# Attention, MoE and routed MoE on one core: the place of the raw weight loads in the attention's load order, and of the routing constants

## The chip, the cores and the metric

One core of one Trainium2 chip. The metric is the device time of one execution in microseconds, as the median of three runs.

## The reference

Three layers follow each other. The attention has 32 heads of 576 rows and 64 columns, with a decay that is a running sum of log f, and a causal mask. Its output, 2304 tokens of 512, goes through a gated MLP ("the first MoE" in the code's names), and that through a routed MoE with eight experts, in which each token goes to one expert.

```python
scores = scale * np.matmul(q, k.transpose(0, 1, 3, 2))
decay = cum[:, :, :, None] - cum[:, :, None, :]
scores = np.where(causal, -1000000000.0, scores + decay)
...
g = x @ w_gate
silu = g * (1.0 / (1.0 + np.exp(-g)))
val = x @ w_val
return (silu * val @ w_out).astype(np.float32)
...
logits = x @ w_gate
e_idx = np.argmax(logits, axis=1)
...
h = np.maximum(x[mask] @ w1[e], 0.0)
ye = h @ w2[e]
out[mask] = gate_w[mask, None] * eom[mask, e, None] * ye
```

## The kernel before, in words

The kernel has three stages on one core. From 0 to about 184 us the attention runs, in 16 pairs of heads; then the first MoE in steps of 384 tokens by 256 hidden columns; from about 680 us on the routing and the eight experts.

In the attention the order of work on every engine is written out by hand, in the table ORDER (lines 38 to 48). Each engine's line is one turn; `Attention.run` (line 346) repeats it once for each pair. An entry such as `qk 1 3` is the operation, the pair relative to the turn, and a tile number: the scores of the next pair, tile 3. TensorE multiplies q and k into PSUM (`qk`, line 164, tiles 4 to 0 in two buffers ps_s), VectorE adds the mask and takes the row maximum (`ttr`, line 180, which empties the PSUM buffer), ScalarE takes the exponential (`exp`, line 188), GpSimd and VectorE make the reciprocal of the row sum (`add`, `rec`, `mul`, lines 196 to 205), TensorE turns the weights (`tr`, line 226), ScalarE and VectorE copy the result (`cp`, lines 235 and 237, tile th), and TensorE multiplies by v (`av`, line 262). VectorE copies the output to xt (line 278); GpSimd splits it into two parts (lines 290 and 288). Every engine works strictly in its order, and so does the queue of SP, which issues the loads.

An entry of the SP line with `> x` is a load that must not be issued before the operation x is done: a hand-made tie that spreads the loads over the turn. `rows` loads rows of the decay (dk, line 142), `load p 0` to `3` are four loads of q and k of a pair (line 132, 144 KB each), `vload` two of v (line 139). q and k are loaded three turns ahead of the pair's own, and their first product is `qk 2 4`, late in the next turn.

The weights of the first MoE come as 64-bit numbers and are decoded to 32 bits on the chip. The first six raw pieces of 512 KB are decoded within the attention, one in every second turn, beginning with the turn of pair 2 (H0). Their loads are `fetch 0 0` to `3`, four quarters of 128 KB each (`quarter`, line 427, tile raw). In the turn after, VectorE does `d0` (line 456) behind the copy `cp 0 0 0`, and `d1` (line 458) at the end; in the turn behind that VectorE does `d2` (460) and ScalarE `sq` (464), and GpSimd finishes (`ts`, `pm1`, `pm2`, lines 466 to 472; `pm3`, 474, a turn later). The later pieces are decoded in the first MoE (`decode`, lines 443 to 448, fetched at line 431).

The routing constants are one tile cst. `Consts.rest` (line 1032) loads 237 KB of it, and `Consts.split` (lines 1036 and 1037) casts two of its 128x128 parts to tile uo on VectorE. They are used by `Route.chunk`, in the last group of the first MoE. In the kernel before, the hook of the first fetch calls `rest`, and that of the first `d0` calls `split`.

In the first MoE each step i has two halves f: `gv` (lines 510 to 518: two products, Tanh, and VectorE's hs and hl), and `g2` (lines 528 to 534: the product ps_y, added to y by VectorE).

Of the kernel before, what the change touches and what calls it, by code (L numbers as in the profile page):

```python
# [33 lines left out]
NP = B * H // 2  # L34
# [7 lines left out]
    DVE="rec 0 1, cp 0 0 0, d2 0, d0 0, ttr 1 3 1, ttr 1 2 1, ttr 1 3 0, ttr 1 2 0, cp 0 1 0, xt -1, "  # L42
        "ttr 1 0 0, ttr 1 1 0, ttr 1 0 1, ttr 1 1 1, cp 0 2 1, rec 1 0, d1 0, ttr 2 4 0, ttr 2 4 1",
    POOL="mul 0 1, sub -2, pm3 -1, ts -1, pm1 0, add 1 0, pm2 0, mul 1 0, add 1 1, cast -1",
    SP="rows 2, load 3 0 > cp 0 0 1, load 3 1 > exp 1 3 1, fetch 0 0 > cp 0 1 1, fetch 0 1 > exp 1 2 1, "
       "load 3 2 > exp 1 3 0, vload 1 0 > cp 0 2 0, fetch 0 2 > exp 1 0 1, vload 1 1 > exp 1 1 1, "
       "load 3 3 > exp 1 0 0, fetch 0 3 > exp 2 4 0",
)
ENG = mybir.EngineType
SYNC = mybir.DependencyInfo(mybir.DependencyClass.Sync, mybir.DependencyReason.DATA)  # L50
# [7 lines left out]
class Attention:  # L58
# [287 lines left out]
    def run(self, hook, pool):  # L346
# [31 lines left out]
        for q in queue.values():  # L378
            q[:] = [o for o in q if o not in done]
        with self.tc.manual_schedule(engines={ENG.PE, ENG.Activation, ENG.DVE, ENG.Pool, ENG.SP}):  # L380
            self.decay(*dec)
# [658 lines left out]
def tile_kernel(tc, io, out, dbg=None):  # L1040
    nc = tc.nc
    with ExitStack() as ctx:
        pool = lambda cx, nm, b=1, **k: cx.enter_context(tc.tile_pool(name=nm, bufs=b, **k))
        cp = pool(ctx, "cst")
        dr = pool(ctx, "dram", space=DRAM)
        per = dict(sb=cp, sb2=cp, dram=dr)
        cst = Consts(nc, cp, io["cst"])
        wts = Weights(nc)
        wts.pools.append(pool(ctx, "wA", 6))
        with ExitStack() as c1:  # L1050
            xp = pool(c1, "x")
            xth = xp.tile([128, 4, N], F32R, name="xth")
            xtl = xp.tile([128, 4, N], F32R, name="xtl")
            raw = pool(c1, "raw", 2)
            tmp = pool(c1, "dtmp", 1)
            m1 = MoE1(tc, c1, cst, io, wts, raw, tmp, xth, xtl)
            with ExitStack() as ca:
                cst.attention(pool(ca, "acst"))
                at = Attention(tc, ca, cst, io, xth, xtl)

                todo, raws = [], {}

                def hook(k, p, j=0):
                    n = (p - H0 - DEC[k]) // 2
                    if k == "fetch":
                        if n == 0 and j == 0:
                            cst.rest()
                            todo.extend(m1.parts(0))
                        if j == 0:
                            raws[n] = raw.tile([128, 1024], I32, name="raw")  # L1070
                        return m1.quarter(raws[n], todo[n][0], j)
                    else:
                        if k == "d0" and n == 0:
                            cst.split()
                        m1.piece(k, raws[n], *todo[n][1:])

                at.run(hook, wts.pools[0])
            m1.open(c1)
            wab = [wts.pools[0], pool(c1, "wB", 6)]
            slp = pool(c1, "slots", space=PSUM)  # L1080
            slots = slp.tile([128, 512], F32, name="slots")
            rt = Route(tc, c1, cst, io, per, m1.y)
            gates = rt.gates(pool(c1, "gtmp"))
            CH = [(384 * i, 384) for i in range(6)]
            CL = CH[:4] + [(1536 + 256 * i, 256) for i in range(3)]
            steps = [(g, t0, n) for g in range(6) for t0, n in (CL if g == 5 else CH)]
            for i in range(len(steps) + 1):
                for f in range(2):
                    if i < len(steps):
                        g, t0, n = steps[i]  # L1090
                        if g < 5 and t0 == 0 and f == 0:
                            wts.pools = [wab[(g + 1) % 2]]
                            if g:
                                m1.load(g + 1)
                        if (i, f) in ((3, 0), (8, 0)):
                            with tc.issue_after(m1.mark[0].ins), tc.issue_after(m1.mark[1].ins):
                                next(gates, None)
                        if i == 1 and f == 0:
                            wts.pools = [wab[1]]
                            todo[:] = m1.parts(1)  # L1100
                        if 2 * i + f in HALF:
                            src, hi, lo = todo.pop(0)
                            with tc.issue_after(m1.mark[0].ins), tc.issue_after(m1.mark[1].ins):
                                m1.decode(m1.fetch(src), hi, lo)
                        if g == 5 and t0 == CH[2][0] and f == 0:
                            wts.pools = [wab[0]]
                            w00 = load_expert(nc, io, wts, raw, 0, 0)
                        m1.gv(g, t0, n, f)
                    if i:
                        for d in (2 * f, 2 * f + 1):  # L1110
                            m1.g2(*steps[i - 1], d)
                if i and steps[i - 1][0] == 5:
                    rt.chunk(*steps[i - 1][1:], slots)
            info = rt.finish(slots)
        with ExitStack() as c2:
            wc = pool(c2, "wC", 12, reuse_waits="tile")
            wts.pools = [wab[0], wc, wc]
            m2 = MoE2(tc, c2, cst, io, wts, rt.yd, rt.gd, info, out)
            pblk = pool(c2, "blk")
            m2.braw = pool(c2, "blk_raw")  # L1120
            cur = cp.tile([128, 1], F32, name="cur")
            nc.vector.memset(cur, 0.0)
            gwk = pool(c2, "gwk")
            m2.L[0, 0] = w00
            with tc.issue_after(rt.mark[0].ins), tc.issue_after(rt.mark[1].ins):
                m2.pull(0)
                m2.warm(WARM[0], info["id1"])
                for t in range(NSB):
                    m2.pre(0, t)
                    m2.warm(WARM[1 + t], m2.YG[0][min(t, 1)])  # L1130
            with tc.issue_after(m2.mark[0].ins), tc.issue_after(m2.mark[1].ins):
                for u in range(1, 4):
                    m2.L[0, u] = load_expert(nc, io, wts, m2.raw, 0, u)
            st = [(e, u) for e in range(E_) for u in range(4)]
            blk = m2.block(pblk, cur, rt, True)
            with tc.manual_schedule(engines={mybir.EngineType.Pool}):
                for i, (e, u) in enumerate(st):
                    if (u == 0 if e else u == P0) and e + 1 < E_:
                        m2.pull(e + 1)
                    if e == 1 and u == 0:  # L1140
                        m2.gates(0)
                    if e and u == 3:
                        m2.gates(e)
                    if i in BLK0:
                        next(blk)
                    m2.g1(e, u)
                    if i == GI:
                        rt.gate_rows(m2.ps_g, gwk)
                        rt.blocks(info, gwk)
                    if u >= P1 and u < P1 + NSB and e + 1 < E_:  # L1150
                        m2.pre(e + 1, u - P1)
                    if i in BLK1:
                        with tc.issue_after(m2.hmark[0].ins), tc.issue_after(m2.hmark[1].ins):
                            next(blk)
                    if i:
                        m2.g2(*st[i - 1])
                    if u < NSB and e:
                        m2.put(e - 1, u)
                    if (e, u) == (6, 3):
                        for _ in blk:  # L1160
                            pass
                nc.gpsimd.drain()
                m2.g2(*st[-1])
                for t in range(NSB):
                    m2.put(E_ - 1, t)
            trip = nc.values_load(info["trip"][0:1, 0:1], min_val=0, max_val=NOB + E_)
            with tc.For_i(0, trip, 1):
                for _ in m2.block(pblk, cur, rt, False):
                    pass
# [35 lines left out]
```

## Time and profile before

| what | value |
|---|---|
| median of 3 runs | 941.75 us (940.64 to 949.98) |
| the profiled execution's own time | 939.82 us |
| its span, first to last instruction | 938.0 us |
| TensorE (PE) busy | 898.9 us, 96% |
| VectorE (DVE) busy | 576.4 us, 61% |
| ScalarE (ACT) busy | 401.0 us, 43% |
| GpSimd (POOL) busy | 242.0 us, 26% |

The busy share of TensorE is an average over the three stages, and TensorE's idle time is not spread evenly; the stretches say where it lies. A wait's row tells which engine stood, at which line, for whom, how long in total, how often and how long at most. In a timeline a row is one or more instructions of a kind; a bracket at the end is the idle time of that engine just before, and what ended it.

### The profile page before, as it was taken

The page shows a single profiled execution, that of the slowest core. Times are in us where ns is not written, and L with a number is a line of the kernel's source. Part 1 is how long each engine was busy: PE and PEld are TensorE (multiplying, and loading weights), DVE is VectorE, ACT ScalarE, POOL GpSimd, SP SyncE. Part 2 cuts the span into 40 slices and gives each one's busy share as a digit, 9 for nine tenths or more (in the row PEclk, how much of TensorE's full clock was granted, in tenths as well). Part 3 has the DMA queues.
Part 4 walks back from the last instruction along what each step waited for, and adds up shares of the span by engine and source line. Part 5 has one row for each costly group of instructions (what it writes and reads, how often), then busy time and mean ns, then how long its engine had stood idle before and what let it go on. Part 6 is the DMA issues. An engine that isn't in the chain of part 4 may idle for free.

```text
span 938.0 us, 23689 instructions
## 1 busy us (share of the span) xinstructions
PE 898.9 (96%) x9848; PEld 862.9 (92%) x9848; DVE 576.4 (61%) x1355; ACT 401.0 (43%) x874; POOL 242.0 (26%) x249
## 2 busy tenths in 40 slices
PE   8988888999999999999999999999899999999995
PEld 6877778899999999999999999999699999999995
DVE  6767776555784396487466445767875556466421
ACT  6766776444431231132132122333365555555421
POOL 2355555711120030020021000000212655155222
PEclk9999999999999999999999999999899999999998
DMA  4433333112230030021021000101595775566300
GB/s 124 137 112 103 107 105 113 51 46 68 70 111 1 1 113 23 1 91 46 1 68 46 1 1 1 68 34 65 177 300 157 234 238 188 172 197 199 114 34 30
DMA packets 59975, 87.87 MB, mean 94 GB/s; under 512 B 7080, under 2 KB 39322, under 8 KB 59867
## 3 DMA queue, kind: packets, MB, share of 16 engines
q1 hardware_dynamic: 54363, 72.17, 25.0%
q0 software_dynamic: 5504, 14.17, 4.3%
q8 instruction: 78, 1.28, 0.5%
q14 instruction: 30, 0.25, 0.1%
HBM read 76.76 MB, written 10.08 MB: 93 GB/s over the span
## 4 chain that ended last, share of the span: by engine, by line
PE 72%; DVE 10%; issue 9%; DMA 4%; POOL 3%; ACT 2%; POOLq 0%; SPq 0%; DVEq 0%; ACTq 0%
PE ps_g L510 27%; PE ps_y L528 14%; PE m_psy L832 8%; PE m_psg L817 7%; PE ps_s L164 4%; PE ps_t L226 4%; PE avx L262 3%; DVE dt L443 2%; DVE e L180 2%; DMA raw<-w 1%; PE rt_ps L668 1%; POOL w L448 1%; POOL out L858 1%; PE m_pst L782 1%; PE m_pst L848 1%
## 5 line engine op out<-in xcount | busy, mean ns | idle before, releaser
L510 PE MATMUL ps_g<-xth,w 128*128 128x384 f32 (+1 forms) x1184 | 309.0, 331 | 0.0
L510 PEld LDWEIGHTS ps_g<-xth,w 128*128 128x128 f32 x1184 | 213.1, 188 | 0.9
L510 PE MATMUL ps_g<-xtl,w 128*128 128x384 f32 (+1 forms) x592 | 196.0, 331 | 0.0
L528 PE MATMUL ps_y<-hh,w 128*128 128x384 f32 (+1 forms) x592 | 160.6, 332 | 2.2 <-DVE y L534 2.2
L817 PE MATMUL m_psg<-ygh,w 128*128 128x304 f32 x512 | 115.1, 307 | 0.4 <-ACT ygh L784 0.4
L832 PE MATMUL m_psy<-h2h,w 128*128 128x304 f32 x512 | 114.6, 306 | 0.0
L448 POOL TENSOR_TENSOR w<-ds,w 128x512 fp32r<-128x512 f32 x30 | 41.6, 1386 | 273.7 <-ACT w L447 273.7
L510 PEld LDWEIGHTS ps_g<-xtl,w 128*128 128x128 f32 x592 | 111.3, 188 | 0.0
L528 PEld LDWEIGHTS ps_y<-hh,w 128*128 128x128 f32 x592 | 107.0, 188 | 4.3 <-DVE y L534 4.0
L188 ACT ACTIVATE e<-e,mx 64x64 f32<-64x64 f32 (+4 forms) x160 | 88.1, 552 | 38.9 <-DVE mx L180 37.9
L744 DVE TENSOR_TENSOR w<-raw,w 128x1024 fp32r<-128x1024 f32 x64 | 76.6, 1222 | 38.0 <-ACT w L743 20.6
L528 PE MATMUL ps_y<-hl,w 128*128 128x384 f32 (+1 forms) x296 | 97.8, 330 | 0.0
L517 ACT ACTIVATE hh<-hs 128x384 fp32r<-128x384 f32 (+1 forms) x74 | 38.2, 516 | 135.9 <-DVE hs L516 135.9
L515 DVE SCALAR_TENSOR_TENSOR hs<-hs,ps_g 128x384 f32<-128x384 f32 (+1 forms) x74 | 40.0, 540 | 83.5 <-ACT hs L514 83.5
L817 PEld LDWEIGHTS m_psg<-ygh,w 128*128 128x128 f32 x512 | 85.5, 189 | 0.6 <-ACT ygh L784 0.5
L832 PEld LDWEIGHTS m_psy<-h2h,w 128*128 128x128 f32 x512 | 85.6, 188 | 0.4
L743 ACT ACTIVATE w<-raw 128x1024 fp32r<-128x1024 f32 x64 | 67.5, 1058 | 39.9 <-PE m_psg L817 17.7
L180 DVE CUSTOM_DVE_ANT_0 e<-ps_s,mask 128x576 f32<-128x576 f32 (+4 forms) x160 | 69.5, 482 | 24.2 <-PE ps_s L164 24.1
L514 ACT ACTIVATE hs<-ps_g 128x384 f32<-128x384 f32 (+1 forms) x74 | 35.4, 478 | 107.2 <-PE ps_g L510 107.1
L534 DVE TENSOR_TENSOR y<-ps_y,y 128x384 f32<-128x384 f32 (+1 forms) x124 | 67.0, 541 | 19.1 <-PE ps_y L528 18.2
L798 POOL DMA_INDIRECT yg<-yd,sl_idx x24 | 27.9, 1163 | 193.6 <-DVE sl_idx L704 168.3
L832 PE MATMUL m_psy<-h2l,w 128*128 128x304 f32 x256 | 77.4, 302 | 0.0
(302 smaller groups left out, 1572.5 us busy)
## 6 DMA issues: line engine op xcount, KB each, us to landing
raw<-w SPq DMA_DIRECT2D x64, 512.0 KB
qk<-qk SPq DMA_DIRECT2D x64, 144.0 KB
raw<-mg SPq DMA_DIRECT2D x10, 512.0 KB
raw<-mv SPq DMA_DIRECT2D x10, 512.0 KB
raw<-mo SPq DMA_DIRECT2D x10, 512.0 KB
yd<-yr SPq DMA_DIRECT2D x18, 256.0 KB
v<-vL SPq DMA_DIRECT2D x16, 160.0 KB
v<-vL SPq DMA_DIRECT2D x16, 128.0 KB
```

Source lines behind the costliest of these rows:

```text
L180: self.nc.vector.tensor_tensor_reduce(out=o, in0=x, in1=y, scale=-0.125, scalar=BIGF, op0=ALU.add, op1=ALU.min, accum_out=mx[:m])
L188: return self.nc.scalar.activation(e, e, ACTF.Exp, bias=self.M.pop((p, i, a))[:m], scale=-1.0, accum_out=self.rs[p % 2][:m, c:c + 1])
L448: nc.gpsimd.tensor_sub(lo, s3, hi.bitcast(F32))
L510: nc.tensor.matmul(ps[:, :n], w[:, k, fs], x[:, k], start=(k == 0 and c == 0), stop=(k == 3 and c == 2))
L515: nc.vector.scalar_tensor_tensor(s[:, :n], s[:, :n], 1.0, pss[0][:, :n], op0=ALU.add, op1=ALU.mult)
L517: a = nc.scalar.activation(hh[:, f, :n], s[:, :n], ACTF.Copy)
L528: nc.tensor.matmul(ps[:, :n], w[:, f, ds], h[:, f, :n], start=(f == 0 and c == 0), stop=(f == 1 and c == 2))
L534: nc.vector.tensor_add(y, ps[:, :n], y)
L743: nc.scalar.activation(hi, r, ACTF.Copy)
L744: nc.vector.tensor_sub(lo, r, hi.bitcast(F32))
L817: nc.tensor.matmul(ps[:, :C], w[:, k, fs], x[:, k], start=(k == 0 and c == 0), stop=(k == 3 and c == 2))
L832: nc.tensor.matmul(self.P[e][d][:, :C], w[:, f, ds], h[:, f], start=(u == 0 and f == 0 and c == 0), stop=(u == 3 and f == 1 and c == 2))
```

## The change

The line of SP in ORDER is written in another order and with other ties: the four quarters of a raw piece stand directly behind `rows`, with the last one tied to `exp 1 2 1`; q's and k's loads and v's stand between and behind them. The load of the constants (`rest`) moves to step 2, second half, of the first MoE, with a dependence on the last load of v; their casts (`split`) move to step 9.

```diff
-    SP="rows 2, load 3 0 > cp 0 0 1, load 3 1 > exp 1 3 1, fetch 0 0 > cp 0 1 1, fetch 0 1 > exp 1 2 1, "
-       "load 3 2 > exp 1 3 0, vload 1 0 > cp 0 2 0, fetch 0 2 > exp 1 0 1, vload 1 1 > exp 1 1 1, "
-       "load 3 3 > exp 1 0 0, fetch 0 3 > exp 2 4 0",
+    SP="rows 2, fetch 0 0 > cp 0 0 1, fetch 0 1 > exp 1 4 1, fetch 0 2 > exp 1 3 1, load 3 0 > cp 0 1 1, "
+       "fetch 0 3 > exp 1 2 1, load 3 1 > exp 1 3 0, vload 1 0 > cp 0 2 0, load 3 2 > exp 1 0 1, "
+       "vload 1 1 > exp 1 1 1, load 3 3 > exp 1 0 0",
...
-                            cst.rest()
...
-                        if k == "d0" and n == 0:
-                            cst.split()
...
+                        if (i, f) == (2, 1):
+                            with tc.issue_after(at.I["vload", NP - 1, 1].ins):
+                                cst.rest()
+                        if (i, f) == (9, 0):
+                            with tc.issue_after(m1.mark[1].ins):
+                                cst.split()
```

On SP's queue, the turn with the first raw piece, before (L427 are the quarters, L132 q and k, L139 v, L142 the decay rows, L1032 the constants):

```order
L132 DMA qk<-qk 128x288 x2
L1032 DMA cst<-cst 128x474
L427 DMA raw<-mg 128x256 x2
L132 DMA qk<-qk 128x288
L139 DMA v<-vL 128x320
L427 DMA raw<-mg 128x256
L139 DMA v<-vL 128x256
L132 DMA qk<-qk 128x288
L427 DMA raw<-mg 128x256
```

And the same turn after the change:

```order
L427 DMA raw<-mg 128x256 x3
L132 DMA qk<-qk 128x288
L427 DMA raw<-mg 128x256
L132 DMA qk<-qk 128x288
L139 DMA v<-vL 128x320
L132 DMA qk<-qk 128x288
L139 DMA v<-vL 128x256
L132 DMA qk<-qk 128x288
```

The four quarters have moved from between the other loads to their head, the last from behind the turn's last load to behind the first, and the constants are gone from here.

On VectorE, the start of the turn behind it, before (L237 is the copy th, L1036 and L1037 the casts of the constants, L456 is d0, L180 the maxima):

```order
L237 COPY th_1096<-ps_t_1043 128x384
L1036 CAST uo<-cst 128x128
L1037 CAST uo<-cst 128x128
L456 TENSOR_SCALAR dt<-raw 128x512
L180 ISA e,mx_1158<-ps_s,mask 128x448
```

After the change, the same place, and the place in the first MoE to which the casts go (L534 adds to y, L518 and L515 are hl and hs):

```order
L237 COPY th_1097<-ps_t_1044 128x384
L456 TENSOR_SCALAR dt<-raw 128x512
L180 ISA e,mx_1101<-ps_s,mask 128x448
...
L534 TENSOR_TENSOR y<-ps_y,y 128x384
L518 TENSOR_TENSOR hl<-hs,hh 128x384
L1036 CAST uo<-cst 128x128
L534 TENSOR_TENSOR y<-ps_y,y 128x384
L1037 CAST uo<-cst 128x128
L515 SCALAR_TENSOR_TENSOR hs<-hs,ps_g 128x384
```

The two casts have left the turn, and d0 follows the copy directly. The order of all other rows of TensorE, VectorE, ScalarE and GpSimd is the same.

## Rows read from the trace of the kernel before

**Rows 1.** Windows: stretch, us, busy us of each engine, PEclk, DMA, GB/s.

```profile
20.00:45.00 25.00, 23.98 (x882) 22.25 (x872) 18.72 (x74) 20.07 (x65) 7.81 (x14) 1.00 0.45 126
...
70.00:95.00 25.00, 20.64 (x677) 18.42 (x675) 18.32 (x68) 16.98 (x53) 13.24 (x16) 1.00 0.35 97
```

**Rows 2.** Waits, 0 to 190 us: total us, times, longest us.

```profile
DVE dt L456 <- DMA raw<-mv: 5.4, 2, 3.1
...
DVE dt L456 <- DMA raw<-mg: 4.0, 2, 3.0
...
DVE dt L456 <- DMA raw<-mo: 2.6, 1, 2.6
...
DVE dt L456 <- issue: 2.1, 1, 2.1
```

**Rows 3.** Timeline of SP, 59 to 68 us: start us, us, instruction.

```profile
59.96 1.56 SPq L427 DMA_DIRECT2D raw<-mg  x2
...
65.66 0.38 SPq L132 DMA_DIRECT2D qk<-qk  x1
66.37 0.33 SPq L427 DMA_DIRECT2D raw<-mg  x1
```

**Rows 4.** Timeline of VectorE (DVE) at four places: start us, us.

```profile
45.76 0.42 DVE L1036 CAST uo<-cst 128x128 fp32r<-128x128 f32 x1
46.10 1.45 DVE L1037 CAST uo<-cst 128x128 fp32r<-128x128 f32 x1
...
66.47 0.56 DVE L237 COPY th<-ps_t 128x384 f32<-128x384 f32 x1 [0.31 <-PE ps_t L226]
70.03 0.43 DVE L456 TENSOR_SCALAR dt<-raw 128x512 int32<-128x512 int32 x1 [3.01 <-DMA raw<-mg]
...
113.59 0.84 DVE L456 TENSOR_SCALAR dt<-raw 128x512 int32<-128x512 int32 x1 [2.30 <-DMA raw<-mv]
...
134.97 1.07 DVE L456 TENSOR_SCALAR dt<-raw 128x512 int32<-128x512 int32 x1 [2.07 <-issue]
```

**Rows 5.** Timeline of TensorE (PE): qk 1 3 (64x448), qk 1 1 (64x192).

```profile
26.16 0.59 PE L164 MATMUL ps_s<-qk 64*64 64x448 f32 x2
...
30.02 0.33 PE L164 MATMUL ps_s<-qk 64*64 64x192 f32 x1
...
44.98 0.59 PE L164 MATMUL ps_s<-qk 64*64 64x448 f32 x2
...
50.61 0.56 PE L164 MATMUL ps_s<-qk 64*64 64x192 f32 x8 [1.38 <-DVE mx L180]
...
66.34 0.59 PE L164 MATMUL ps_s<-qk 64*64 64x448 f32 x2
...
72.10 0.56 PE L164 MATMUL ps_s<-qk 64*64 64x192 f32 x8 [1.27 <-DVE mx L180]
...
155.09 0.59 PE L164 MATMUL ps_s<-qk 64*64 64x448 f32 x2
...
160.39 0.56 PE L164 MATMUL ps_s<-qk 64*64 64x192 f32 x8 [0.38 <-DVE mx L180]
```

**Rows 6.** Timeline of ScalarE (ACT), 60 to 62 us (exp 1 2 1).

```profile
60.54 0.55 ACT L188 ACTIVATE e<-e,mx 128x320 f32<-128x320 f32 x1
```

**Rows 7.** Timeline of VectorE in the first MoE, 290 to 312 us.

```profile
301.18 0.56 DVE L515 SCALAR_TENSOR_TENSOR hs<-hs,ps_g 128x384 f32<-128x384 f32 x1 [2.11 <-ACT hs L514]
```

**Rows 8.** Timeline of GpSimd (POOL) at three places.

```profile
46.05 1.41 POOL L288 TENSOR_TENSOR xtl<-xt,xth 128x576 fp32r<-128x576 f32 x1
...
66.81 1.41 POOL L288 TENSOR_TENSOR xtl<-xt,xth 128x576 fp32r<-128x576 f32 x1
68.19 1.26 POOL L474 TENSOR_TENSOR w<-ds,w 128x512 fp32r<-128x512 f32 x1
...
134.49 1.27 POOL L474 TENSOR_TENSOR w<-ds,w 128x512 fp32r<-128x512 f32 x1
```

**Rows 9.** Timeline of TensorE, 140 to 143 us.

```profile
141.60 0.70 PE L262 MATMUL avx<-th,v 64*64 64x256 f32 x11 [1.47 <-issue]
```

## Prediction

> **What bounds the kernel now.** I read the busy time by stretches first. From 20 to 45 us, before any raw weight is decoded, TensorE is busy 23.98 us of 25; from 70 to 95 us, in the turns that also decode, 20.64 us, at the same granted clock of 1.00 [rows 1]. So the attention stage loses TensorE time that it does not lose without the decoding, and the clock is not the reason. The waits over the first 190 us come next: VectorE stood 4.0 + 5.4 + 2.6 us, in five waits, for the transfers of raw, and 2.1 us in a sixth that the trace only labels issue, all in front of line 456, which is d0, the first step of a decode [rows 2]. That is 14.1 us for six decodes. The reason is in the queue of SP and in VectorE's own rows: the fourth quarter of a piece is issued at 66.37, the copy th ends at 67.00, and d0, the next instruction of VectorE, starts at 70.03 [rows 3, 4]. Every row of VectorE behind it, the score maxima first, waits with it.
>
> What this costs TensorE is in its rows. In a turn without decode the product qk 1 3 starts at 26.16 and qk 1 1 at 30.02, 3.86 us later. In the six turns with d0 that distance is 5.63 in the first, 5.76 in the second and 5.30 in the last, and 5.8 to 5.9 in the three between; qk 1 1 waits there for VectorE's maximum, which frees its PSUM buffer [rows 5].
>
> **The change part by part.** *The four quarters go first.* Today the fourth is tied to the exponential 2 4 0, ScalarE's last of a turn. Now it is tied to exp 1 2 1, which in the turn that ends with these rows is done at 61.09, read-out aside [rows 6]. It is issued at once, for q's load 3 0 in front of it hangs on an earlier copy. With the longest delay from issue to d0 that rows 3 and 4 show, 66.37 to 70.03 or 3.7 us, it has landed by 65, and VectorE is not ready for it before 67.0: 2 us to spare. So the wait goes, six times. What is late next? From d0's start to qk 1 1 it takes 72.10 - 70.03 = 2.07 us. With d0 at 67.0 VectorE would allow qk 1 1 at 69.07; TensorE by its own 3.86 us reaches it at 66.34 + 3.86 = 70.20. So TensorE is next, with 1.1 us of cover. The gain by its rows is the sum of the six distances less six times 3.86: 34.2 - 23.2 = 11.0 us. VectorE's rows give the upper end: 14.1 us of waits.
>
> *q, k and v behind them.* Each transfer of q and k is needed more than a turn after its issue: that of 65.66 feeds a product behind the qk 1 1 of 72.10, over 6.4 us later [rows 3, 5], and its last part keeps its place. Later loads in a turn cost nothing as long as landing stays near 3.7 us. The queue carries the same bytes in a turn, less 237 KB of constants once.
>
> *Constants.* Their load leaves the first of the decoding turns for a place behind the last v, where SP next has a weight piece of the MoE. The two casts leave VectorE in the first decode turn, where they last from 45.76 to 47.55, 1.8 us [rows 4]. They stand ahead of d0 and are part of the first turn's 5.63 already, so I add them to the upper end alone: 15.9 us. In the first MoE the casts stand on both sides of an add of y. VectorE idles 2.11 us there before its next row, in each half step, waiting for ScalarE [rows 7]; 1.8 us fit into that. I take 0; without the cover it is 1.8 us once.
>
> *A lock that the wait now hides.* d0 took 0.43 us at 70.03, but 0.84 at 113.59 and 1.07 at 134.97 [rows 4]; that last time GpSimd ran a product from 134.49 to 135.76, and d0 ended 0.28 us behind it [rows 8]. The second cast took 1.45 us while GpSimd ran its subtraction of 1.41 us from 46.05. So d0 does not run beside such a row of GpSimd. With the wait gone, d0 at 67.0 meets the subtraction of 66.81 (to 68.22), and behind that the product of 68.19 (to 69.45) [rows 8]. If d0 gets in between the two, it ends at 68.50, as if it had started at 68.07, and allows qk 1 1 at 70.14, just inside TensorE's 70.20: nothing lost. The Trainium skill (SBUF — State Buffer, "Who interferes with whom") calls the port pair of the two engines an exclusive lock: whoever issues first holds it for the whole instruction and the other blocks. That agrees with these rows, and speaks against the change, since it puts d0 under GpSimd's two rows. What no row shows plainly is who gets the pair between two back-to-back rows of GpSimd; the first cast did start before the subtraction that was next, and ended ahead of it. So I take it that d0 gets in.
>
> **Sum.** Between 11.0 and 15.9 us, with the lock toward the lower end; I take 12, near TensorE's own rows, since it is next in line. The rest, from 184 us, is TensorE's and only starts earlier. The profiled execution has a span of 938.0 us and took 939.82; less 12 it would have 926 and 927.8. The median of the three runs is 1.9 us higher, 941.75, so I forecast 941.75 - 12 = 929.75, or 929.7.
>
> **Rivals.** *The lock holds through both rows.* If d0 must let the subtraction and the product pass, it ends at 69.45 + 0.28 = 69.73, as from 69.30, and qk 1 1 comes at 71.37: 0.7 us gained of 1.9. The first turn has no such product and gains 1.2; the third and the last, taken like the second, gain 0.7 each; the fourth and fifth, where d0 ran 0.84 and 1.07 us behind the product already, gain nothing. Sum 3.3, time 938.4. For it: the 1.07 us row. Against it: the first cast.
>
> *More is freed.* With VectorE ahead, the gaps labelled issue also shrink: the full 15.9 us, 925.9. For it: those gaps occur only in turns with raw traffic. Against it: TensorE is next at 70.20 whatever VectorE does.
>
> *TensorE starves for instructions.* In the decoding turns TensorE stops with nothing that it waits for, 1.47 us in the longest case [rows 9], while from 20 to 45 us, mostly ahead of the raw loads, all its idle time is 1.0 us [rows 1]. If these are late instruction fetches, four quarters in a burst delay them more. At one more such gap of 1.47 in each of six turns, 8.8 us are given back: 938.6, no change. It decides against the change from 2.0 us a turn on (12 / 6); at 3 us it is 18 us, 947.8, slower. Against it: two quarters already go out together, at 59.96 [rows 3], and the bytes of a turn stay.
>
> *It does not do what it says.* If the fourth quarter landed 2 us later than by the rows, d0 would wait as now; then the time stays at about 940.
>
> **How the numbers follow.** Forecast 0.58; more freed 0.14; lock through both rows 0.13; starving that eats most of it 0.08, and more than all of it 0.03; hidden nothing 0.04. About 1% is what a measurement of this kernel can tell from no change: 932.3 below, 951.2 above. The first two cases lie below 932.3, with a tenth of the forecast's weight above it: 0.67. Some of the lock's turns may go one way and some the other, which leaves a little of that case below as well: 0.70 faster, 0.28 within, 0.02 slower, most of the slower case being smaller than 9.4 us. The range runs from 924.5, the full 15.9 and a little, to 938.5, the two cases of no change.
>
> **What would show it.** Right: the waits of line 456 for raw are gone; qk 1 3 to qk 1 1 is near 3.9 us in the six turns; d0 lasts 0.4 to 1.8 us and starts within 0.6 us of the copy th; the first MoE starts about 12 us earlier than now. The lock rival shows as d0 of over 2 us or a gap before it with GpSimd busy, and qk 1 1 still waiting for VectorE. Starving shows as gaps labelled issue that are longer or more frequent in the turns with raw loads. Wrong in any case would be a first MoE that starts 12 us earlier and an end that does not.

## The result and the profile after

The kernel before has a median of 942.56 us over 8 runs of this comparison (940.64 to 949.98), the changed kernel 933.92 us (931.79 to 937.95). The ratio is 0.9906, with a 95% interval of 0.9878 to 0.9935: 8.6 us less, or 0.94%, where 12 us were forecast. The time lies in the predicted range, and the interval of the gain reaches to both sides of the 1% that the prediction took as its bound for faster. The profiled span goes from 938.0 to 930.0 us, at a mean granted clock of 0.99; both profiles are of the shortest execution of their kernel.

The wait that the change aims at is gone. Of the four rows of [rows 2] none is left: no wait of VectorE at line 456 stands in the list. What TensorE waited for is read from its own rows of the same view. First the kernel before, 0 to 190 us (total us, times, longest us):

```profile
PE ps_s L164 <- DVE mx L180: 9.1, 9, 1.4
...
PE ps_t L226 <- issue: 5.7, 9, 1.3
...
PE avx L262 <- issue: 2.8, 3, 1.5
...
PE ps_s L164 <- issue: 0.3, 1, 0.3
```

And the changed kernel:

```profile
PE ps_t L226 <- issue: 5.3, 12, 0.8
...
PE ps_s L164 <- DVE mx L180: 2.5, 3, 1.3
...
PE avx L262 <- issue: 2.1, 3, 1.1
...
PE ps_s L164 <- issue: 0.6, 2, 0.3
```

The wait for VectorE's maxima has fallen from 9.1 to 2.5 us. The gaps labelled issue, in which the trace shows nothing that TensorE waits for, have hardly changed: 8.8 us in 13 before, 8.0 us in 17 after. They come back below, since they are now the larger part.

SP's queue in the turn that [rows 3] show (start us, us, instruction) has three quarters in one row and the fourth at 61.19, where it was 66.37. VectorE's rows at the place of [rows 4] have d0 directly behind the copy th, with no bracket:

```profile
57.32 2.30 SPq L427 DMA_DIRECT2D raw<-mg  x3
59.98 1.12 SPq L132 DMA_DIRECT2D qk<-qk  x1
61.19 0.38 SPq L427 DMA_DIRECT2D raw<-mg  x1
```

```profile
66.43 0.56 DVE L237 COPY th<-ps_t 128x384 f32<-128x384 f32 x1
66.90 0.42 DVE L456 TENSOR_SCALAR dt<-raw 128x512 int32<-128x512 int32 x1
67.62 0.62 DVE L180 CUSTOM_DVE_ANT_0 e<-ps_s,mask 128x448 f32<-128x448 f32 x1 [0.30 <-PE ps_s L164]
...
146.71 1.18 DVE L456 TENSOR_SCALAR dt<-raw 128x512 int32<-128x512 int32 x1
...
283.36 0.22 DVE L1036 CAST uo<-cst 128x128 fp32r<-128x128 f32 x1
...
283.96 0.22 DVE L1037 CAST uo<-cst 128x128 fp32r<-128x128 f32 x1
```

The row behind d0 at 67.62 now waits for TensorE: the roles are turned round. The two casts take 0.22 us each in the first MoE and nothing waits for them. GpSimd's rows, which answer to [rows 8], tell who had to wait there:

```profile
66.98 1.63 POOL L288 TENSOR_TENSOR xtl<-xt,xth 128x576 fp32r<-128x576 f32 x1
...
146.19 1.41 POOL L288 TENSOR_TENSOR xtl<-xt,xth 128x576 fp32r<-128x576 f32 x1
```

At 66.90 d0 was first and GpSimd's subtraction took 1.63 us instead of 1.41; at 146.71 d0 was second and took 1.18 us. TensorE's rows, to be read with [rows 5], give the distance from qk 1 3 to qk 1 1:

```profile
66.25 0.59 PE L164 MATMUL ps_s<-qk 64*64 64x448 f32 x2
...
70.33 0.33 PE L164 MATMUL ps_s<-qk 64*64 64x192 f32 x1
...
146.06 0.59 PE L164 MATMUL ps_s<-qk 64*64 64x448 f32 x2
...
150.46 0.33 PE L164 MATMUL ps_s<-qk 64*64 64x192 f32 x1
```

In the six turns with d0 it is now 4.12, 4.08, 4.41, 4.10, 4.06 and 4.40 us, together 25.2 where they were 34.2. In the windows, as in [rows 1], the stretch from 70 to 95 us has gained 2.27 us of TensorE's time:

```profile
70.00:95.00 25.00, 22.91 (x778) 21.04 (x782) 18.93 (x71) 19.09 (x62) 15.12 (x20) 1.00 0.42 119
```

The attention's last copy to xt starts at 175.21 instead of 184.03, 8.8 us earlier, and the routing's index row (line 704) at 661.56 instead of 669.97, 8.4 us earlier. So the whole difference arises in the attention; of its 8.8 us the span keeps 8.0.

### The profile page after: what moved, and what is told of

Same layout as the page of the kernel before. It is cut to its first block, busy times and chain, and to the rows that moved or that the text cites. A ratio compares the mean times of both kernels' runs of the same rounds, so it can differ in the third digit from the quotient of the medians.

```text
span 930.0 us, 23697 instructions
## 1 busy us (share of the span) xinstructions
PE 899.3 (97%) x9848; PEld 864.0 (93%) x9848; DVE 577.0 (62%) x1355; ACT 402.6 (43%) x874; POOL 242.7 (26%) x249
## 3 DMA queue, kind: packets, MB, share of 16 engines
q8 instruction: 78, 1.28, 0.6%
## 4 chain that ended last, share of the span: by engine, by line
PE 77%; issue 8%; DVE 7%; POOL 3%; DMA 2%; ACT 1%; POOLq 0%; SPq 0%; DVEq 0%; ACTq 0%
PE ps_g L510 27%; PE ps_y L528 14%; PE m_psy L832 8%; PE m_psg L817 8%; PE ps_s L164 6%; PE ps_t L226 5%; PE avx L262 4%; DVE dt L443 2%; DMA raw<-w 1%; PE rt_ps L668 1%; POOL w L448 1%; POOL out L858 1%; PE m_pst L782 1%; PE m_pst L848 1%; DVE ds L445 1%
## 5 line engine op out<-in xcount | busy, mean ns | idle before, releaser
L515 DVE SCALAR_TENSOR_TENSOR hs<-hs,ps_g 128x384 f32<-128x384 f32 (+1 forms) x74 | 40.0, 541 | 83.3 <-ACT hs L514 83.3
L180 DVE CUSTOM_DVE_ANT_0 e<-ps_s,mask 128x576 f32<-128x576 f32 (+4 forms) x160 | 70.2, 485 | 25.0 <-PE ps_s L164 19.2
L534 DVE TENSOR_TENSOR y<-ps_y,y 128x384 f32<-128x384 f32 (+1 forms) x124 | 67.0, 541 | 19.1 <-PE ps_y L528 18.2
```

The costliest lines, as they stand in the source:

```text
L180: self.nc.vector.tensor_tensor_reduce(out=o, in0=x, in1=y, scale=-0.125, scalar=BIGF, op0=ALU.add, op1=ALU.min, accum_out=mx[:m])
L534: nc.vector.tensor_add(y, ps[:, :n], y)
```

## The experiments

Ratios are to the kernel before, run beside each kernel on the same chip, with 95% intervals. A turn is counted from qk 1 3 to the next qk 1 3; turns 4, 6, ... 14 are those with d0.

### The load order taken apart

These four share a kernel before of 943.52 us.

**Quarters first, the rest as before.** The four quarters go ahead, q's, k's and v's loads keep the ties of before, the constants stay in the attention.

```diff
+"rows 2, load 3 0 > cp 0 0 1, fetch 0 0 > cp 0 0 1, fetch 0 1 > exp 1 4 1, load 3 1 > exp 1 3 1,
+ fetch 0 2 > exp 1 3 1, fetch 0 3 > exp 1 2 1, load 3 2 > exp 1 3 0, vload 1 0 > cp 0 2 0, ..."
```

> The four quarters go to the head of the turn as in the change, but q's, k's and v's loads keep the ties of before, and the constants stay in the attention. Theory A (the waits of line 456 were the whole gain, about 10.6 us over the six turns with d0, and the later q, k and v loads gave about 1.2 us of it back in the first three turns): 1 us faster than the changed kernel less what the two casts cost, so 931.5 to 933.5, with the first three turns as long as before (8.3, 8.8, 10.0 us). Theory B (the burst of four quarters makes the loss, the ties of the others nothing): no better than the changed kernel, 934 to 936, for the burst stays and the casts return.

Measured: 934.73 us, 0.9901 (0.9883 to 0.9919), the ratio of the change. So the quarters alone give the gain, and neither the later loads nor the constants' new place adds to it or takes from it beyond some 2 us. The time is the one that Theory B gave; the cause that Theory B names, the burst, is looked at in the run without raw traffic.

**Only the later loads.** q, k and v get the ties of the changed kernel; the quarters stay late.

```diff
+"rows 2, load 3 0 > cp 0 1 1, fetch 0 0 > cp 0 1 1, fetch 0 1 > exp 1 2 1, load 3 1 > exp 1 3 0, vload 1 0 > cp 0 2 0,
+ load 3 2 > exp 1 0 1, fetch 0 2 > exp 1 0 1, vload 1 1 > exp 1 1 1, load 3 3 > exp 1 0 0, fetch 0 3 > exp 2 4 0"
```

> Only the ties of q's, k's and v's loads of the changed kernel; the quarters keep theirs, and the constants stay. Theory A: 1 to 2 us slower than before, 943.5 to 944.5, from the first three turns. Theory B: no difference, 942 to 943. Under both, VectorE waits about 14 us for raw as before.

Measured: 946.99 us, 1.0035 (1.0017 to 1.0052). It is slower by more than either theory said, and the waits in front of d0 (line 457 in this file) have grown from 14.1 to 17.2 us. SP's queue and VectorE's row in the second of these turns, where they grew most:

```profile
66.41 0.42 SPq L428 DMA_DIRECT2D raw<-mg  x1
...
67.91 0.35 SPq L428 DMA_DIRECT2D raw<-mg  x1
```

```profile
72.49 0.43 DVE L457 TENSOR_SCALAR dt<-raw 128x512 int32<-128x512 int32 x1 [4.20 <-DMA raw<-mg]
```

The whole turn stands 1.3 us later here: the copy th ends at 68.29, where it was 67.02. Against th the last quarter is issued only 0.3 us later than in [rows 3], but the third some 1.6 us later, so that the two go out 1.50 us apart instead of 2.88. d0 starts 4.58 us behind the last issue instead of 3.66, and waits 1.2 us more. In the other five turns the wait differs by -0.3 to 0.9 us.

What the 3.3 us of time are made of is not shown. The six distances from qk 1 3 to qk 1 1 are only 1.1 us longer together. In this execution the granted clock was also at 0.5, the lower of its two levels (1.2 and 2.4 GHz), from 74.5 to 77.9 us, behind two stops of TensorE in that same turn (0.76 and 1.64 us); the rest of the attention has 1.00. Later ties of loads in no hurry cost time here, while hurried ones stand among and behind them; how much of it is d0's longer wait stays open.

**Only the constants.** Load order of before, constants loaded and cast in the first MoE.

```diff
-                            cst.rest()
...
-                            cst.split()
...
+                            with tc.issue_after(at.I["vload", NP - 1, 1].ins):
+                                cst.rest()
```

> Only the constants move to the first MoE; the load order is that of before. If the casts were hidden behind the wait for raw: d0 of the first turn waits longer, 0 to 1 us faster, 941.5 to 942.5. If they cost their 1.8 us: 940.8 or less. The first MoE keeps its length within 0.5 us under both.

Measured: 944.06 us, 1.0001 (0.9983 to 1.0020). The 1.8 us of casts lay under the wait: the first d0, which stood 0.99 us behind them in the kernel before, now stands 2.63:

```profile
49.93 0.43 DVE L457 TENSOR_SCALAR dt<-raw 128x512 int32<-128x512 int32 x1 [2.63 <-DMA raw<-mg]
```

**The wait put back.** The changed kernel, with the fourth quarter last again and tied as before.

```diff
-... > cp 0 1 1, fetch 0 3 > exp 1 2 1, load 3 1 > exp 1 3 0, ...
+... load 3 3 > exp 1 0 0, fetch 0 3 > exp 2 4 0"
```

> The changed kernel, but its fourth quarter is tied to the exponential 2 4 0 again and stands last in the turn. If the wait for that quarter is the cause of the gain: VectorE waits 12 to 14 us at line 456 again and the time is 941 to 944, all of the gain gone. If the order of the other quarters and loads had a part in it, part of the gain stays: 936 to 940.

Measured: 944.56 us, 1.0013 (0.9996 to 1.0030). All of the gain is gone, and the waits are back, 13.9 us in the six turns:

```profile
DVE dt L456 <- DMA raw<-mv: 5.3, 2, 2.9
...
DVE dt L456 <- DMA raw<-mo: 4.1, 2, 3.1
...
DVE dt L456 <- DMA raw<-mg: 2.8, 1, 2.8
...
DVE dt L456 <- DMA dk<-cd: 1.7, 1, 1.7
```

The place and the tie of one load, the fourth quarter, carry the whole difference between the two kernels, within the error. The last row names the decay rows' load, which merely came last by the profile.

### What holds the rest back

These four share a kernel before of 945.93 us. The changed kernel, run again beside them:

> The changed kernel itself, as the measure for the others of this group: 933 to 935, 0.990 to 0.992 of before. A second profile of it shows how far the length of a turn moves between executions of the same program: if the first three turns differ by over 0.5 us from the first profile, their loss there was scatter.

It took 939.89 us, 0.9932 (0.9910 to 0.9955), more than expected. That is the yardstick for the other three; the two intervals of the change together reach from 0.988 to 0.996.

Its profile (span 939.6 us) shows how far two executions of one program lie apart. The attention's last copy to xt starts at 180.29 instead of 175.21; the third turn takes 11.4 us instead of 10.6, turns 9 to 14 take 61.5 instead of 59.4, and the gaps labelled issue are 12.5 us in 20 instead of 8.0 in 17. From the routing's index row to the end it takes 273.2 us instead of 268.4: TensorE stands 2.93 us for VectorE's h2l (line 820) there, where the first execution has 0.41, and in that stop the granted clock falls to 0.5, the lower level, from 697.6 to 704.4 us, where the first has 1.00. So two or three microseconds between two versions need not come from their load orders.

**The last two quarters alone.** The kernel before, with only those two a little earlier.

```diff
-"... fetch 0 2 > exp 1 0 1, vload 1 1 > exp 1 1 1, load 3 3 > exp 1 0 0, fetch 0 3 > exp 2 4 0"
+"... fetch 0 2 > cp 0 2 0, fetch 0 3 > exp 1 0 1, vload 1 1 > exp 1 1 1, load 3 3 > exp 1 0 0"
```

> The kernel before, with only the last two quarters moved, by about one and four exponentials: the third is issued with v's first load and the fourth after exp 1 0 1, about 3 us earlier than before; everything else, the constants too, as before. If only the landing of the fourth quarter counts: issued about 4 us ahead of d0 it lands just in time, waits of line 456 of 0 to 3 us in all, and the time is that of the changed kernel within 1.5 us. If the place at the head of the turn has a part of its own: half of the gain or less, 937 to 941.

Measured: 937.89 us, 0.9917 (0.9896 to 0.9938), 2.0 us below the changed kernel beside it and the gain of the change within the error, although 2.0 us of waits for raw are left and d0, now behind GpSimd's row in four turns, lasts 1.1 to 1.4 us in them:

```profile
DVE dt L456 <- DMA raw<-mo: 1.2, 2, 0.8
...
DVE dt L456 <- DMA raw<-mg: 0.6, 1, 0.6
...
DVE dt L456 <- DMA raw<-mv: 0.2, 1, 0.2
```

So the last two or three microseconds of VectorE's delay are worth nothing measurable: something else is next.

**q, k and v early again.** The changed kernel with the ties of before for q, k and v, the SP line of the first experiment.

> The changed kernel with q's, k's and v's loads at the ties of before and the quarters between them. If later loads cost 1 to 2 us: 932 to 933, faster than the changed kernel. If they cost nothing once the quarters go ahead: the changed kernel's time within 1 us.

Measured: 936.69 us, 0.9904 (0.9888 to 0.9921), 3.2 us below the changed kernel beside it, which neither theory said. In the two profiles, 4.5 us apart in span, the attention's last copy to xt differs by 0.9 us (180.29 and 179.38), and 3.6 us lie behind the routing's index row, where this execution has no second stretch of the lower clock. So with the quarters ahead no cost of later loads is shown in the attention; the medians alone would not exclude 1 to 3 us.

**No raw traffic.** The changed kernel, with the third to the sixth piece not loaded: their decodes read the first two again. The weights of the first MoE differ by that, so the routing does, and the total is not comparable; only the attention's turns are read.

```diff
...
+                        if n >= 2:
+                            raws[n] = raws[n - 2]
+                            return None
```

> The changed kernel without the loads of raw pieces 2 to 5 in the attention: their decodes read pieces 0 and 1 again, so the weights of the first MoE are others, while all other work stays. If raw traffic starves TensorE (its gaps labelled issue): turns 7 to 14 become 0.4 to 1 us shorter each, the total 3 to 8 us below the changed kernel, and the gaps in these turns go. If the traffic costs nothing once it lands in time: the changed kernel's time within 1 us, and the gaps stay.

From turn 9 on no raw load runs. The six turns 9 to 14 took 59.8 us, and 59.4 and 61.5 us in the two executions of the changed kernel; in the kernel before they took 64.8. The gaps labelled issue are 6.0 + 2.9 + 1.8 us, between the 8.0 and 12.5 of those two, and they stand in turns 9 to 14 too. So raw transfers, in a burst or not, are not what makes these gaps, and cost the six turns no more than the 2 us by which those executions differ.

### Is it the decoding at all?

These share a kernel before of 945.33 us.

**No decode.** The third to the sixth piece are neither loaded nor decoded in the attention, and the first MoE takes the first two in their place; its total too is not comparable. It was executed once.

```diff
...
+                    if n >= 2:
+                        return None
...
+                            g = m1.W[0][0]
+                            m1.W[0] = [g, g, tuple(t.rearrange("p (a b) c -> p a (b c)", a=2) for t in g)]
```

> The changed kernel without loading and decoding raw pieces 2 to 5 in the attention; all weights of the first MoE's first group come from pieces 0 and 1, so the routing is another and only the attention's turns are read. If the work of the decodes on VectorE, ScalarE and GpSimd sets the turns: turns 7 to 14 shrink from 10 to 9 us or less. If TensorE with its gaps sets them: they stay at 9.5 to 10 us.

TensorE's rows show the start of qk 1 3 in turn 9 and behind turn 14, first in the changed kernel, then without decode, there also the two distances to qk 1 1 in turns 13 and 14:

```profile
96.55 0.59 PE L164 MATMUL ps_s<-qk 64*64 64x448 f32 x2
...
155.98 0.59 PE L164 MATMUL ps_s<-qk 64*64 64x448 f32 x2
```

```profile
100.22 0.59 PE L164 MATMUL ps_s<-qk 64*64 64x448 f32 x2
...
140.04 0.59 PE L164 MATMUL ps_s<-qk 64*64 64x448 f32 x1
...
143.96 0.33 PE L164 MATMUL ps_s<-qk 64*64 64x192 f32 x1
...
149.61 0.59 PE L164 MATMUL ps_s<-qk 64*64 64x448 f32 x2
...
154.03 0.33 PE L164 MATMUL ps_s<-qk 64*64 64x192 f32 x1
...
160.11 0.59 PE L164 MATMUL ps_s<-qk 64*64 64x448 f32 x2
```

59.43 and 59.89 us: without any decoding work on VectorE, ScalarE and GpSimd the six turns are no shorter than in the changed kernel's first execution, and 1.6 us shorter than in its second. So the decoding costs the six turns no more than those two differ, and no order of the raw loads can be expected to give much more. The distance from qk 1 3 to qk 1 1 is 3.92 us in turn 13 and 4.42 in turn 14, and so it goes by turns in all six (3.86, 4.35, 3.92, 4.34, 3.92, 4.42): every second turn, the one in which d0 would stand, is longer although nothing is decoded.

**d0 moved, in both kernels.** d0 goes from behind the copy `cp 0 0 0` to the end of VectorE's turn, in the changed kernel and, in a second run, in the kernel before, whose loads and constants stay as they were.

```diff
-... cp 0 0 0, d2 0, d0 0, ttr 1 3 1, ... rec 1 0, d1 0, ttr 2 4 0, ttr 2 4 1
+... cp 0 0 0, d2 0, ttr 1 3 1, ... rec 1 0, d0 0, d1 0, ttr 2 4 0, ttr 2 4 1
```

> The changed kernel, with d0 moved on VectorE from behind the copy cp 0 0 0 to the end of the turn, just ahead of d1, where VectorE waits about 1.3 us for qk 2 4. If GpSimd's lock on d0 (0.4 to 1.6 us in a turn) costs time: 1 to 3 us faster than the changed kernel. If TensorE is what is late next and d0's place is covered: the changed kernel's time within 1 us.

> The kernel before with that move of d0 alone: no load and no constant moves, and the fourth quarter is issued last as before. If VectorE's wait at d0's place is the whole cause, the same gain comes without any change of the loads: 0.990 to 0.993 of before. If the order of the loads matters by itself: less than half of it.

Measured: 938.68 us, 0.9927 (0.9907 to 0.9948), and 937.68 us, 0.9908 (0.9877 to 0.9940). In the kernel before that one move gives the gain of the change, within the error, with the quarters as late as ever: the last is still issued at 66.85, but d0 runs when it has long landed, without a wait and clear of GpSimd's rows. By line, the six d0 in it (ns at least, median, at most):

```profile
L456 DVE TENSOR_SCALAR dt<-raw x6: 376/379/414, 54.2 to 156.8; 128x512 int32<-128x512 int32 x6
```

In the changed kernel the move brings nothing further that can be measured (0.9927, against 0.9906 and 0.9932 without it). So no cost of the lock, which made d0 up to 1.18 us long in the profile above, is seen.

**Fewer warm products.** TensorE starts with products of a tile of zeros (line 125). Here the changed kernel has WARM0 at 2 instead of 10, eight of them fewer, each two products and two weight loads in the trace, to see whether the gaps labelled issue belong to places of the program.

```diff
-H0, WARM0, WARM1 = 2, 10, 3
+H0, WARM0, WARM1 = 2, 2, 3
```

> The changed kernel with 2 warming products at the start in place of 10, so that every later instruction of TensorE stands 32 places (16 matmuls, 16 weight loads) earlier in its stream. If the gaps labelled issue belong to block boundaries of the stream (254 recorded instructions lie between one and the next): the gap that stands ahead of the last 27 matmuls of tr 0 2 near 62 us stands about 16 matmuls later in the program, and the others likewise. If they belong to an operation or a transfer: they keep their places. Time within 2 us of the changed kernel under both.

Measured: 938.71 us, 0.9925 (0.9901 to 0.9949). The gaps lie at other places of the program, but behind the same number of instructions. The gap that stands ahead of the last 27 products of tr 0 2 in the changed kernel stands ahead of the last 11 here, 16 products later, as forecast:

```profile
61.95 0.63 PE L226 MATMUL ps_t<-d,e 64*64 64x64 f32 x27 [0.34 <-issue]
```

```profile
64.87 0.40 PE L226 MATMUL ps_t<-d,e 64*64 64x64 f32 x11 [0.59 <-issue]
```

The windows from the start of the span to just before a gap show the number: the count of products stands behind PE's busy time, that of weight loads behind PEld's. The kernel before:

```profile
0.00:41.13 41.13, 36.56 (x978) 30.66 (x978) 28.89 (x108) 30.70 (x87) 11.29 (x27) 1.00 0.46 124
...
0.00:158.33 158.33, 137.85 (x4393) 122.04 (x4394) 111.24 (x404) 110.49 (x336) 81.19 (x112) 1.00 0.42 118
```

The changed kernel:

```profile
0.00:42.42 42.42, 36.44 (x978) 30.59 (x978) 28.98 (x107) 30.79 (x87) 11.30 (x27) 1.00 0.44 119
...
0.00:149.06 149.06, 136.41 (x4391) 121.77 (x4391) 112.56 (x407) 112.10 (x338) 82.69 (x112) 1.00 0.44 124
```

Fewer warm products:

```profile
0.00:45.05 45.05, 35.52 (x978) 28.53 (x978) 29.19 (x108) 30.81 (x87) 11.28 (x27) 1.00 0.42 113
...
0.00:155.98 155.98, 135.91 (x4391) 119.81 (x4391) 115.07 (x411) 113.01 (x340) 82.50 (x112) 1.00 0.43 118
```

978 + 978 = 1956 instructions stand ahead of the first of these gaps in all three, and 8782 to 8787 ahead of the second; at one between them (83.43, 81.87 and 85.01 us) it is 4484 to 4486. Between neighbouring gaps lie 250 to 255 recorded instructions or a multiple of that. From the first of the two gaps to the second the kernel before took 117.2 us, the changed one 106.6.

## Why the prediction was right and wrong

**Right: what bounds, and what the change removes.** VectorE stood for the fourth quarter in front of d0, and TensorE behind it for the maximum. All six waits went; the wait put back took the gain with it; and moving d0 instead of the loads gave the same, within the error. d0 starts as th ends, within the 0.6 us that the prediction named.

**Not contradicted: "Later loads in a turn cost nothing".** The changed kernel and the one with early q, k and v end the attention 0.9 us apart in their profiles; their ratios are 0.9932 and 0.9904, with intervals that overlap. The condition belongs to it: with the quarters still behind them, the later loads cost 3.3 us.

**Right: the constants at 0.** Moved alone they change nothing measurable (0.9983 to 1.0020), since the wait took their place in the attention. In the first MoE they cost two rows of 0.22 us under idle time.

**Right in the outcome, different in the detail: the lock.** d0 was to "get in" between GpSimd's two rows. In five of six turns it ran ahead of both, in 0.42 to 0.62 us, and in one behind the subtraction. In a second execution of the changed kernel it stood at 88.80 for 1.62 us, behind a subtraction of 88.72 (1.42 us) and ended 0.33 us into the product that began at 90.09; this is the case of the prediction. It waited through both rows nowhere, so the rival of 938.4 falls. Moving d0 clear of GpSimd brought nothing measurable, so no cost of the lock is seen either way. The Trainium skill (SBUF — State Buffer, "Who interferes with whom") has the pair as an exclusive lock; the longer row on whichever side came second agrees with it.

**Wrong: the size.** 8.6 us were measured, 8.0 in the profiled spans, for a forecast of 12. The step that failed is "TensorE by its own 3.86 us". That is the distance in a turn without d0, and it does not hold for the others: in the six d0 turns TensorE's own distance came out at 4.06 to 4.41, 25.2 us in all instead of 23.2, so this term freed 9.0 us instead of 11.0. It is not d0 that stretches them. With d0 moved to the end of the turn in the kernel before they add up to 25.8 us, and without any decode turns 10, 12 and 14 took 4.34 to 4.42.

What stretches them is in the starts of TensorE's products. In each of the six turns there is one place between qk 1 3 and qk 1 1, on the grid of instructions that the last section tells of, at which the next product starts 0.20 to 0.54 us after the one before, where its neighbours start at most 0.15 us apart. The six make 2.29 us, about the 2.0 us that the term lacked. In two of them the trace calls this a gap (0.31 and 0.32 us). In the others the product ahead is still busy by the profile, whose ends are modelled, and only the counts show that nothing starts, as here for 0.30 us:

```profile
0.00:69.60 69.60, 62.46 (x1863) 53.89 (x1863) 50.02 (x181) 51.46 (x151) 28.45 (x48) 1.00 0.43 120
0.00:69.90 69.90, 62.76 (x1863) 53.89 (x1863) 50.32 (x183) 51.76 (x152) 28.69 (x48) 1.00 0.43 119
```

In turns 7, 9, 11 and 13, without d0, the grid's place between these products takes 0.05 to 0.11 us, and the distance is 3.76 to 3.87 us.

The rest of the error is in what lies around the distance. "I take 12" put one microsecond on top of TensorE's own rows, toward VectorE's 15.9. The balance by turns is closed: the whole d0 turns fell from 70.4 to 59.8 us, 10.6 less, 9.0 of it in the distance above and 1.6 beside it; the six fetch turns went from 60.1 to 60.4, the first two from 17.1 to 17.8, and what follows the last turn from 18.5 to 19.2 us. 10.6 - 0.3 - 0.7 - 0.7 = 8.9, and the last xt came 8.8 us earlier. So the added microsecond came, and 1.7 us were lost elsewhere, which the sum put at nothing. In the first two turns only q's, k's and v's loads have moved, and these turns take 17.1 to 19.0 us in the runs of this study, so I don't read a cause into them. The balance is of one execution each: in the second one of the changed kernel the d0 turns took 62.0 us, the fetch turns 63.1, and the six distances 26.5.

**Half right: TensorE's gaps.** The rival was that TensorE "starves for instructions", more so by a burst of quarters. The burst is refuted as their cause, by the run without traffic and by the one without decode, which have the gaps at the same counts. But the gaps are real, and they go by the count of instructions. In the kernel before some of them lay under the wait for the maximum. One place in both kernels shows it, in front of the same qk 1 1; before:

```profile
92.08 1.10 PE L262 MATMUL avx<-th,v 64*64 64x256 f32 x22 [0.56 <-issue]
94.13 0.56 PE L164 MATMUL ps_s<-qk 64*64 64x192 f32 x8 [0.95 <-DVE mx L180]
```

And after:

```profile
89.75 1.08 PE L262 MATMUL avx<-th,v 64*64 64x64 f32 x21 [0.31 <-issue]
90.59 0.33 PE L164 MATMUL ps_s<-qk 64*64 64x192 f32 x1
```

Before, the gap of 0.56 was followed by 0.95 us of waiting for VectorE, so it cost nothing. After, the gap of 0.31 is followed by no wait: qk 1 1 comes when the products ahead of it are through, and the distance is the longest of the six, 4.41. What such a gap takes should have been left in the sum, as time that TensorE needs for itself.

**Open.** That the gaps set the floor of some 9.9 us a turn is argued, not shown: they are there in all variants, and the variants without traffic and without decode reach the same floor; but no run took the gaps away. Why their sum moves between 8.0 and 12.5 us in two executions of one program is open too. I don't know why some boundaries show no gap, or why the first ones stay hidden. Nor did a version beat the change clearly: quarters first, the last two quarters, early q, k and v, and d0 moved in either kernel lie at 0.990 to 0.993, with overlapping intervals.

## What to carry to other kernels

When a wait is to be removed, look for the engine that is next over all turns and several executions, not in the best turn, and count the gaps that the wait now covers: they come out when it goes. A hand-made tie of one load can be worth as much as a whole order of loads, and the same wait can be removed at the other end, by moving its consumer to a place where the data have landed. Where loads share a queue, the hurried ones belong ahead: later ties of the others cost 3.3 us here while the hurried ones stood behind them, and nothing that was shown once these were ahead. And profile the same program twice before reading a few microseconds as the effect of an edit: here two executions differed by more than the edits that were compared.

## What the runs showed of the hardware

TensorE's unexplained gaps in the attention came at fixed counts of its instructions: behind 1956, 3220 to 3221, 4484 to 4486 and 8782 to 8787 recorded products and weight loads in all three kernels shown above, 0.3 to 1.0 us each there, and the others that the trace lists lie on the same grid of 250 to 255. The run without decode has them there too. Two turns hold some 1280 of these instructions and five steps of the grid 1264, so the gaps fall at nearly the same places of every second turn. Because of that they look like a property of the turns with raw traffic, and I had taken them for one.

The row of instruction transfers fits (packets, MB, share of 16 engines), for the whole execution of the changed kernel and for 42.42 to 149.06 us:

```profile
q8 instruction: 78, 1.28, 0.6%
```

```profile
q8 instruction: 27, 0.44, 1.7%
```

1.28 MB in 78 packets are 16.4 KB each. The execution has 9848 products and 9848 weight loads, 252.5 to a packet; the stretch has 6826 of them, 252.8 to a packet. The Trainium skill (Runtime: NRT & Kernel Launch, "Instruction fetch mechanics") says that an engine's instructions are refilled by a DMA queue of its own in blocks of 16 KiB, 256 instructions, and that the cost of crossing a block is mostly hidden. The block agrees with the grid: five steps of it hold 1264 products and weight loads and, in the trace's records, 16 semaphore instructions of TensorE's sequencer, which the counts above leave out; 1280 in all, 256 to a step. That each gap is such a refill is read from these counts; no run changed the refill. The other half of the page's sentence, the hidden cost, doesn't hold for this stage: it issues some 64 TensorE instructions in a microsecond (6826 in 106.6 us), and in the changed kernel 17 gaps on the grid, between 38 and 153 us, leave TensorE idle for 8.0 us in all.
